# A fused attention and two MLPs: the second MLP's first chunk without the seven-product form, and a weight decoded between the two halves of a pair

## The chip, the cores and the metric

The kernel runs on one core of one Trainium2 chip. The metric is the device time of one execution in microseconds; three runs of the kernel before gave 1170.4 to 1173.76 us, median 1173.32 us. Lower is better.

## The reference

Attention with rotary embedding over 4 x 8 heads of 576 x 64, then two MLPs on the 2304 x 512 result. All of it is float32. What matters here are the MLPs:

```python
def _moe_ref(x, w_gate, w_val, w_out):        # 512 -> 1536 -> 512
    gate = 1.0 / (1.0 + np.exp(-(x @ w_gate)))
    val = x @ w_val
    return (gate * val @ w_out).astype(np.float32)

def _moe2_ref(x, w_in, w_out):                # 512 -> 2048 -> 512
    h = x @ w_in
    g = h * (1.0 / (1.0 + np.exp(-1.702 * h)))
    return (g @ w_out).astype(np.float32)
```

## The kernel before

The weights come from memory as 64-bit floats, seen as pairs of 32-bit words. Every float32 operand of a matmul is split into a high and a low part, and each product is made of three matmul sweeps (low by high, high by low, high by high; `split_mm`, L545).

**Tiles and chunks.** The 2304 tokens are five blocks n = 0 to 4: four of 512 and one of 256. Each MLP runs over chunks of 256 hidden columns (`FFC`): the first MLP has six chunks, (1, 0) to (1, 5), the second eight, (2, 0) to (2, 7). In a chunk, a block has a hidden step ("h", `hidden`, 48 matmuls in the first MLP, which has a gate and a value matrix, 24 in the second) and an output step ("2", `second`, 24 matmuls of 512 columns; 12 for the last block in the second MLP, or 24 of 256 columns in the first), whose results VectorE adds into `acc[n]` from four PSUM buffers (`ps_o`). `out1` (L702) is the first MLP's output step, `out2` (L721) the second's. In the last chunk of the first MLP `out1` also makes the next MLP's input of each block, with ScalarE for the high part and GpSimd for the low one (`split_x`, L105).

**Pairs.** Blocks 0 and 1 of a chunk are made together ("P" for the gate, or for the second MLP's only matrix, and "Q" for the value) by a seven-product form of a 2 x 2 block product (`hidden_pair`, L627): 7 products of 6 matmuls instead of 48 matmuls. It needs four sums of blocks 0 and 1 (`pair_sums`, L610: four VectorE operations on 1024 columns, four ScalarE copies, four VectorE low parts), made once per MLP, and differences of weights (`differences`, L199, on GpSimd; their casts on ScalarE and GpSimd are held back in the list `ready` until "r", or until a pair, takes them). Chunk (1, 0) makes its blocks plainly; all others pair. After its last product a pair still has a tail on VectorE and ScalarE (`step`, L659) that ends in the parts of `g` that the output steps read.

**Weights.** Each decode ("d", L929) takes the next piece (128 x 512 values, 512 KB as loaded) of a single list over all chunks: ScalarE (L182), five VectorE operations (L189 to L195), GpSimd for the low part (L217), then the issue of the next load. There is one `raw` buffer (L158), so that load waits until VectorE has read the old piece (L191). A chunk of the first MLP has 4 input pieces and 2 of w_out, one of the second 2 and 2. `w_out` of the first MLP has one buffer, so it can be decoded only when the last output step of the chunk before has been made.

**Order.** All engines work strictly in the order of the program text. The order of a chunk is written out as a string in `plans` (L967), where "s" does not occur yet:

```python
1: "P 2 Q d d h 2 d h d 2 r h d 2 d 2",
"last": "P 2 Q d d h 2 d h d 2 r h 2 d 2",
"first": "P 2 d h 2 d h 2 d h r d 2 d 2",
2: "P 2 d h 2 d h r 2 d h 2 d 2",
```

"last" is chunk (1, 5), "first" is (2, 0). Output steps wait in a queue, `pend`: "2" takes the oldest. At the start of each paired chunk one is left over from the chunk before, that of block 4, and the "2" behind P takes that one. `pair_sums` for the second MLP is called in `out1` right after block 1 of chunk (1, 5) (L719). The new `acc` of the second MLP comes from the same four buffers as the old one, and takes one whose old tile nothing will read again.

Of the kernel before, what the change touches and what calls it, by code (L numbers as in the profile page):

```python
# [11 lines left out]
AF = mybir.ActivationFunctionType  # L12
ALU = mybir.AluOpType
# [3 lines left out]
P = 128  # L17
# [9 lines left out]
def f(ap):  # L27
    return ap.bitcast(F32)
# [3 lines left out]
def attention_then_mlps(  # L32
# [20 lines left out]
    nc = tc.nc  # L53
# [5 lines left out]
    KT = DM // P  # L59
# [21 lines left out]
    first = keep.tile([P, 2 * KT * BLK], F32, tag="xhl0", name="first", bufs=1)  # L81
# [12 lines left out]
    xf = {}  # L94
    acc = {}

    def new_xhl(n):
        xhl[n] = mlp["x", (n + 1) // 2].tile([P, 2, KT, width[n]], F32R, tag=f"xhl{n}", name=f"xhl{n}", bufs=1)

    def new_f32(n, name):  # L100
        return big.tile(
            [P, KT * width[n]], F32, tag=f"f32_{width[n]}", name=f"{name}{n}", bufs=width.count(width[n])
        )

    def split_x(n, e, src, eng):  # L105
        a = src.rearrange("p (e w) -> p e w", w=width[n])[:, e, :]
        nc.scalar.activation(xhl[n][:, 0, e, :], a, AF.Copy)
        eng.tensor_tensor(xhl[n][:, 1, e, :], a, f(xhl[n][:, 0, e, :]), ALU.subtract)
# [17 lines left out]
    class Weights:  # L126
# [37 lines left out]
        def decode(self, i, act=False):  # L164

            if i < self.n_in and i % 2 == 0:
                self.w[i // 2] = self.half(big if i else self.pool, i // 2)
            if i >= self.n_in and self.o is None:  # L170
                where, tag = (big, "w_in1") if self.kind == 2 and self.c % 2 == 0 else (big, "w_out")
                self.o = where.tile([P, 2, MT * DM], F32R, tag=tag, name="w_out", bufs=1)
            w, at = (self.w[i // 2], i % 2) if i < self.n_in else (self.o, i - self.n_in)
            w = w[:, :, at * PIECE : (at + 1) * PIECE]
            raw = self.raw.pop(i)
            low, high = raw[:, :, 0], raw[:, :, 1]
            c = stage[0].tile([P, PIECE], U32, tag="wc", name="wc", bufs=1)
            t = stage[0].tile([P, PIECE], U32, tag="wt", name="wt")
            self.t[i] = t
            V = nc.vector  # L180
            return [
                lambda: nc.scalar.activation(f(c), f(high), AF.Copy, scale=2.0**-112),  # L182
                (
                    lambda: V.scalar_tensor_tensor(
                        f(c), f(c), LARGEST, least[:, 0:1].to_broadcast([P, PIECE]), op0=ALU.min, op1=ALU.max
                    )
                )
                if act
                else lambda: V.tensor_scalar(f(c), f(c), LARGEST, -LARGEST, op0=ALU.min, op1=ALU.max),  # L189
                lambda: V.tensor_scalar(t, c, 3, 0x7FFFFFF8, op0=ALU.logical_shift_left, op1=ALU.bitwise_and),  # L190
                lambda: V.scalar_tensor_tensor(t, low, 29, t, op0=ALU.logical_shift_right, op1=ALU.bitwise_or),  # L191
                lambda: V.scalar_tensor_tensor(t, c, 0x80000000, t, op0=ALU.bitwise_and, op1=ALU.bitwise_or),  # L192
                (lambda: nc.scalar.activation(w[:, 0, :], f(t), AF.Copy))
                if act
                else lambda: V.tensor_copy(w[:, 0, :], f(t)),  # L195
                lambda: self.lo(w, t),
            ] + ([lambda: self.differences(i // 2)] if i % 2 == 1 and i < self.n_in and (self.kind, self.c) != (1, 0) else [])

        def differences(self, m):  # L199
            t = [f(self.t.pop(2 * m + i)) for i in range(2)]  # L200
# [344 lines left out]
    def split_mm(ps, l, r, n):  # L545

        for sl, sr in ((1, 0), (0, 1), (0, 0)):
            for a in range(n):
                nc.tensor.matmul(  # L549
                    ps, l(sl, a), r(sr, a), start=(sl == 1 and a == 0), stop=(sl + sr == 0 and a == n - 1)  # L550
                )
# [49 lines left out]
    def pair_todo(at):  # L601
        a, b = (at[n].rearrange("p (h c) -> p h c", h=2) for n in range(2))
        return (
            ("S1", b[:, 1], b[:, 0], b[:, 1], ALU.add),
            ("S3", b[:, 0], a[:, 0], b[:, 0], ALU.subtract),
            ("S2", a[:, 0], b[:, 1], a[:, 0], ALU.subtract),
            ("S4", a[:, 1], a[:, 1], a[:, 0], ALU.subtract),
        )

    def pair_sums(todo):  # L610
        to = []
        for name, out_, x, y, op in todo:
            nc.vector.tensor_tensor(out_, x, y, op)
            if name == "S3":
                sums[:] = [mlp["s"].tile([P, 2, 6, BLK], F32R, tag="sums", name="sums", bufs=1)]
            t, e = (xhl[1], 0) if name == "S1" else (sums[0], 2 * "S2 S3 S4".split().index(name))
            to.append(t[:, :, e : e + 2, :].rearrange("p s e c -> p s (e c)"))
            nc.scalar.activation(to[-1][:, 0], out_, AF.Copy)
        for (_, x, *_), t in zip(todo, to):
            nc.vector.tensor_tensor(t[:, 1], x, f(t[:, 0]), ALU.subtract)  # L620

    def pair_room(kind):
        if kind == 1:
# [56 lines left out]
    def hidden(kind, W, n):  # L680
        g = mlp["p"].tile([P, 2, MT, BLK], F32R, tag="g", name="g", bufs=3)[:, :, :, : width[n]]
        for m in range(MT):
            hidden_m(kind, W, n, m, g)
        return g

    row_runs = []
    for t in range(NT // P):
        runs = []
        c = 0
        while c < P:  # L690
            b, j = divmod(t * P + c, S)
            if j < MAIN:
                ch, p0 = divmod(j, P)
                n = min(P - c, P - p0)
                runs.append((c, n, b * S + MAINC * p0 + ch, MAINC))
            else:
                n = min(P - c, S - j)
# [4 lines left out]
    def out1(c, nchunk, W, n, g):  # L702
        if c == 0:
            acc[n] = new_f32(n, "acc")
        wd = width[n]
        if c == nchunk - 1:
            new_xhl(n)
        for e in range(KT):
            ps = mlp["ps_o"].tile([P, 512], F32, tag="pso", name="pso")
            split_mm(ps[:, :wd], lambda s, m: W.w_out(s, m, e * P, P), lambda s, m: g[:, s, m, :], MT)  # L710
            a = acc[n].rearrange("p (e w) -> p e w", w=wd)[:, e, :]
            if c == 0:
                nc.vector.tensor_copy(a, ps[:, :wd])
            else:
                nc.vector.tensor_tensor(a, ps[:, :wd], a, ALU.add)  # L715
            if c == nchunk - 1 and (n != 1 or e >= KT // 2):
                split_x(n, e, acc[n], nc.gpsimd)
        if c == nchunk - 1 and n == 1:
            pair_sums(pair_todo(acc))  # L719

    def out2(c, nchunk, W, n, g):  # L721
        if c == 0:
# [123 lines left out]
    def split_block(n):  # L846
        for e in range(KT):
            if (n, e) not in split_done:
                split_e(n, e)

    with tc.manual_schedule():
# [72 lines left out]
        def next_load():  # L924
            if stream:
                key, i = stream[0]
                wts[key].load(i)
# [17 lines left out]
        for n in range(NBLK):  # L945
            if n + 1 < NBLK:
                split_block(n + 1)
            if n == 0:
                for i in range(W.done, W.n):
                    if i not in W.raw:  # L950
                        W.load(i)
                    for op in W.decode(i):
                        op()
                next_load()
            g = hidden_rest(W) if n == 0 else hidden(1, W, n)
            if n == 1:
                pair_sums(pair_todo(xf))
            if n == 4:
                ready.pop()()
                decode()  # L960
            if n:
                second()
            put(1, 0, n, g)
            if n > 1:
                decode()

        plans = {  # L967
# [4 lines left out]
        }  # L972
        for kind, c in chunks[1:]:
            W = wts[kind, c]
            plan = {(1, FF1 // FFC - 1): "last", (2, 0): "first"}.get((kind, c), kind)
            n = 2
            for op in plans[plan].split():
                if op == "r":
                    while ready:
                        ready.pop()()  # L980
                elif op == "P":
                    room = pair_room(kind)
                if op in "PQ":
                    for m, g in enumerate(hidden_pair(kind, W, "PQ".index(op), room)):
                        put(kind, c, m, g)
                elif op == "2":
                    second()
                elif op == "d":
                    decode()
                elif op == "h":  # L990
                    put(kind, c, n, hidden(kind, W, n))
                    n += 1
# [110 lines left out]
```

## Time and profile before

| | us |
|---|---|
| median of three runs | 1173.32 |
| the profiled execution, its time | 1172.27 |
| the same, its span | 1170.1 |
| TensorE busy (5988 matmuls) | 1115.5 (95%) |
| VectorE busy | 826.6 (71%) |
| ScalarE busy | 463.7 (40%) |
| GpSimd busy | 350.5 (30%) |

The span runs from the first to the last instruction. The attention comes first; chunk (1, 1) begins at 358.33 us, the second MLP at 767.93 us and its second chunk at 828.70 us. A TensorE busy time counts matmuls at either clock, so that a slow stretch is busy too. Times in the rows below are us from the span's start; a row of the timeline may stand for several instructions of a kind (x48).

### The profile page before, as it was taken

The page shows a single profiled execution, that of the slowest core. Times are in us where ns is not written, and L with a number is a line of the kernel's source. Part 1 is how long each engine was busy: PE and PEld are TensorE (multiplying, and loading weights), DVE is VectorE, ACT ScalarE, POOL GpSimd, SP SyncE. Part 2 cuts the span into 40 slices and gives each one's busy share as a digit, 9 for nine tenths or more (in the row PEclk, how much of TensorE's full clock was granted, in tenths as well). Part 3 has the DMA queues.
Part 4 walks back from the last instruction along what each step waited for, and adds up shares of the span by engine and source line. Part 5 has one row for each costly group of instructions (what it writes and reads, how often), then busy time and mean ns, then how long its engine had stood idle before and what let it go on. Part 6 is the DMA issues. An engine that isn't in the chain of part 4 may idle for free.

```text
span 1170.1 us, 15833 instructions
## 1 busy us (share of the span) xinstructions
PE 1115.5 (95%) x5988; PEld 926.4 (79%) x5988; DVE 826.6 (71%) x1418; ACT 463.7 (40%) x929; POOL 350.5 (30%) x333
## 2 busy tenths in 40 slices
PE   8999999999998899899998998698999999999998
PEld 7778888887787788787787887577788888888887
DVE  7887887877775656565556565676787777787864
ACT  5777877775522222222222222342223333243321
POOL 5445455412315032140130323352131230321300
PEclk9999999999999899899898998899899999999999
DMA  6676667621101110110111101011121111211114
GB/s 210 179 211 169 196 173 193 152 58 55 37 20 53 36 55 18 54 54 19 54 36 37 44 29 55 18 33 40 48 61 37 37 54 37 54 37 37 54 36 127
DMA packets 35804, 85.05 MB, mean 73 GB/s; under 512 B 6289, under 2 KB 11025, under 8 KB 33937
## 3 DMA queue, kind: packets, MB, share of 16 engines
q1 hardware_dynamic: 34912, 83.33, 24.8%
q8 instruction: 47, 0.77, 0.3%
q10 hardware_dynamic: 816, 0.72, 0.2%
q14 instruction: 29, 0.23, 0.1%
HBM read 60.44 MB, written 4.72 MB: 56 GB/s over the span
## 4 chain that ended last, share of the span: by engine, by line
PE 74%; DVE 13%; POOL 3%; ACT 3%; DMA 3%; issue 2%; SPq 0%; DVEq 0%; ACTq 0%; POOLq 0%
PE pso L549 25%; PE psh L549 16%; PE psh L636 14%; PE ps_x L518 5%; PE ps_p L487 4%; PE pss L415 4%; PE pss L416 3%; POOL wt L205 2%; DMA raw<-in_moe_w_out_dram 2%; DVE wt L191 2%; DVE g L671 1%; DVE wt L192 1%; PE ps_x L515 1%; DVE wc L189 1%; DVE wt L190 1%
## 5 line engine op out<-in xcount | busy, mean ns | idle before, releaser
L549 PE MATMUL psh<-xhl,w_in 128*128 128x512 f32 (+1 forms) x1488 | 293.1, 355 | 2.5 <-ACT gf L579 2.5
L549 PEld LDWEIGHTS psh<-xhl,w_in 128*128 128x128 f32 x1488 | 248.5, 189 | 43.2 <-ACT gf L579 3.0
L549 PE MATMUL pso<-w_out,g 128*128 128x512 f32 (+1 forms) x870 | 205.9, 393 | 8.0 <-DVE acc L732 5.8
L549 PEld LDWEIGHTS pso<-w_out,g 128*128 128x128 f32 x870 | 164.6, 191 | 43.4 <-DVE acc L732 6.2
L549 PE MATMUL pso<-g,w_out 128*128 128x512 f32 (+1 forms) x720 | 169.7, 394 | 30.7 <-POOL w_out L217 18.3
L549 PEld LDWEIGHTS pso<-g,w_out 128*128 128x128 f32 x720 | 135.7, 204 | 61.0 <-POOL w_out L217 20.4
L217 POOL TENSOR_TENSOR w_in<-wt,w_in 128x512 fp32r<-128x512 f32 x38 | 49.2, 1294 | 362.9 <-DVE w_in L195 334.8
L418 DVE TENSOR_REDUCE nm<-pss 128x1 f32<-128x576 f32 x144 | 108.4, 753 | 31.1 <-PE pss L416 30.2
L433 ACT ACTIVATE P<-pss,nm 128x576 f32<-128x576 f32 x128 | 94.8, 741 | 48.5 <-DVE nm L418 34.3
L581 ACT ACTIVATE g<-gf 128x512 fp32r<-128x512 f32 (+1 forms) x88 | 49.6, 564 | 154.6 <-DVE gf L580 152.9
L582 DVE TENSOR_TENSOR g<-gf,g 128x512 fp32r<-128x512 f32 (+1 forms) x88 | 60.0, 681 | 55.5 <-ACT g L581 55.5
L217 POOL TENSOR_TENSOR w_out<-wt,w_out 128x512 fp32r<-128x512 f32 x28 | 36.0, 1285 | 209.6 <-DVE w_out L195 209.6
L579 ACT ACTIVATE gf<-psh 128x512 f32<-128x512 f32 (+1 forms) x88 | 45.9, 522 | 116.4 <-PE psh L549 116.3
L734 DVE TENSOR_TENSOR acc<-pso,acc 128x512 f32<-128x512 f32 (+1 forms) x127 | 80.7, 680 | 11.5 <-PE pso L549 10.7
L580 DVE TENSOR_TENSOR gf<-psh,gf 128x512 f32<-128x512 f32 (+1 forms) x88 | 52.8, 600 | 48.4 <-PE psh L549 29.0
L305 POOL TENSOR_TENSOR x<-x,rope_sb 128x576 f32<-128x576 f32 x56 | 78.3, 1419 | 3.7 <-DMA x<-in_qk_dram 3.7
L487 PE MATMUL ps_p<-ident,P 128*128 128x128 f32 x576 | 78.4, 275 | 0.0
L715 DVE TENSOR_TENSOR acc<-pso,acc 128x512 f32<-128x512 f32 (+1 forms) x100 | 59.2, 632 | 21.1 <-PE pso L549 21.0
L487 PEld LDWEIGHTS ps_p<-ident,P 128*128 128x128 f32 x576 | 65.6, 141 | 8.0 <-issue 6.3
L182 ACT ACTIVATE wc<-raw 128x512 f32<-128x512 f32 x66 | 43.5, 659 | 69.8 <-DMA raw<-in_moe_w_out_dram 33.6
L518 PE MATMUL ps_x<-PT,v 128*64 128x320 f32 (+1 forms) x512 | 69.4, 412 | 0.0
L473 ACT ACTIVATE PT<-ps_p 128x512 f32<-128x512 f32 (+2 forms) x126 | 64.2, 534 | 4.4 <-PE ps_p L487 4.3
(124 smaller groups left out, 1726.7 us busy)
## 6 DMA issues: line engine op xcount, KB each, us to landing
x<-in_qk_dram SPq DMA_DIRECT2D x14, 1152.0 KB, 5.8
raw<-in_moe_w_out_dram SPq DMA_DIRECT2D x28, 512.0 KB, 3.5
raw<-in_moe_w_in_dram SPq DMA_DIRECT2D x16, 512.0 KB, 3.7
raw<-in_moe_w_val_dram SPq DMA_DIRECT2D x12, 512.0 KB, 3.9
raw<-in_moe_w_gate_dram SPq DMA_DIRECT2D x10, 512.0 KB, 3.8
v<-in_v_dram SPq DMA_DIRECT2D x16, 256.0 KB, 3.5
Z<-X SPq DMA_DIRECT2D x14, 288.0 KB, 3.0
Z<-Y SPq DMA_DIRECT2D x14, 288.0 KB, 3.7
```

What stands on the lines that cost most here:

```text
L217: nc.gpsimd.tensor_tensor(w[:, 1, :], f(t), f(w[:, 0, :]), ALU.subtract)
L305: eng.tensor_tensor(x, x, rope_sb[:, t, c * S : (c + 1) * S], ALU.mult)
L418: nc.vector.tensor_reduce(nm, ps[:, :, :HALF], axis=AX.XY, op=ALU.max, negate=True)
L433: nc.scalar.activation(st[i]["P"][j][:, c : c + S].rearrange("p (n c) -> p n c", n=2), ps[:, :, :HALF], AF.Exp, bias=nm, accum_out=st[i][" ...
L473: nc.scalar.activation(dst, src, AF.Copy)
L487: nc.tensor.transpose(ps[:, (2 * x + y) * P : (2 * x + y + 1) * P], st[i]["P"][2 * a + y][:, c * P : (c + 1) * P], ident,)
L518: nc.tensor.matmul(ps[h * D : (h + 1) * D, :n], vt[:, h * MAINC + t, :], PT[:, h * (MAINC + 1) + t, :], start=False, stop=(t == MAINC - 1),)
L549: nc.tensor.matmul(ps, l(sl, a), r(sr, a), start=(sl == 1 and a == 0), stop=(sl + sr == 0 and a == n - 1))
L582: nc.vector.tensor_tensor(g[:, 1, m, :], gf, f(g[:, 0, m, :]), ALU.subtract)
L636: nc.tensor.matmul(ps, W.block(i, w, sl, kk), pair_x(x, sr, kk), start=start and first, stop=end, skip_group_check=not start,)
L715: nc.vector.tensor_tensor(a, ps[:, :wd], a, ALU.add)
L734: nc.vector.tensor_tensor(a, ps, a, ALU.add)
```

## The change

Chunk (2, 0) makes blocks 0 and 1 by plain hidden steps, so it needs no weight differences (the condition in `decode`: `self.c` instead of all but (1, 0)). `pair_sums` becomes a generator in five steps: "s" in the plan of (2, 0) takes one. `out1` no longer calls it, and splits all four parts of block 1. Where chunk (1, 0) decodes the pieces of (1, 1) is moved up by half a block. In chunks (1, 1) to (1, 5) one decode of the own w_out moves from behind Q to before it, and the second one stays behind it. Chunk (1, 5) decodes one piece more, without "r"; chunk (2, 0) has six "2" instead of five.

```diff
@@ -194,7 +194,7 @@
                 if act
                 else lambda: V.tensor_copy(w[:, 0, :], f(t)),
                 lambda: self.lo(w, t),
-            ] + ([lambda: self.differences(i // 2)] if i % 2 == 1 and i < self.n_in and (self.kind, self.c) != (1, 0) else [])
+            ] + ([lambda: self.differences(i // 2)] if i % 2 == 1 and i < self.n_in and self.c else [])
 
         def differences(self, m):
             t = [f(self.t.pop(2 * m + i)) for i in range(2)]
@@ -607,17 +607,21 @@
             ("S4", a[:, 1], a[:, 1], a[:, 0], ALU.subtract),
         )
 
-    def pair_sums(todo):
-        to = []
-        for name, out_, x, y, op in todo:
+    def pair_sums(at):
+        low = None
+        for name, out_, x, y, op in pair_todo(at):
             nc.vector.tensor_tensor(out_, x, y, op)
             if name == "S3":
                 sums[:] = [mlp["s"].tile([P, 2, 6, BLK], F32R, tag="sums", name="sums", bufs=1)]
             t, e = (xhl[1], 0) if name == "S1" else (sums[0], 2 * "S2 S3 S4".split().index(name))
-            to.append(t[:, :, e : e + 2, :].rearrange("p s e c -> p s (e c)"))
-            nc.scalar.activation(to[-1][:, 0], out_, AF.Copy)
-        for (_, x, *_), t in zip(todo, to):
-            nc.vector.tensor_tensor(t[:, 1], x, f(t[:, 0]), ALU.subtract)
+            t = t[:, :, e : e + 2, :].rearrange("p s e c -> p s (e c)")
+            nc.scalar.activation(t[:, 0], out_, AF.Copy)
+            if low:
+                nc.vector.tensor_tensor(*low)
+            low = t[:, 1], out_, f(t[:, 0]), ALU.subtract
+            yield
+        nc.vector.tensor_tensor(*low)
+        yield
 
     def pair_room(kind):
         if kind == 1:
@@ -713,10 +717,8 @@
                 nc.vector.tensor_copy(a, ps[:, :wd])
             else:
                 nc.vector.tensor_tensor(a, ps[:, :wd], a, ALU.add)
-            if c == nchunk - 1 and (n != 1 or e >= KT // 2):
+            if c == nchunk - 1:
                 split_x(n, e, acc[n], nc.gpsimd)
-        if c == nchunk - 1 and n == 1:
-            pair_sums(pair_todo(acc))
 
     def out2(c, nchunk, W, n, g):
         if c == 0:
@@ -954,30 +956,38 @@
                 next_load()
             g = hidden_rest(W) if n == 0 else hidden(1, W, n)
             if n == 1:
-                pair_sums(pair_todo(xf))
-            if n == 4:
+                for _ in pair_sums(xf):
+                    pass
+            elif n == 2:
+                decode()
+            elif n == 3:
                 ready.pop()()
+            elif n == 4:
                 decode()
             if n:
                 second()
             put(1, 0, n, g)
-            if n > 1:
+            if n in (2, 3):
                 decode()
 
         plans = {
-            1: "P 2 Q d d h 2 d h d 2 r h d 2 d 2",
-            "last": "P 2 Q d d h 2 d h d 2 r h 2 d 2",
-            "first": "P 2 d h 2 d h 2 d h r d 2 d 2",
+            1: "P 2 d Q d h 2 d h d 2 r h d 2 d 2",
+            "last": "P 2 d Q d h 2 d h d 2 h d 2 d 2",
+            "first": "h 2 h s 2 s d h s 2 d h s r 2 d h s 2 d 2",
             2: "P 2 d h 2 d h r 2 d h 2 d 2",
         }
         for kind, c in chunks[1:]:
             W = wts[kind, c]
             plan = {(1, FF1 // FFC - 1): "last", (2, 0): "first"}.get((kind, c), kind)
-            n = 2
+            n = 0 if c == 0 else 2
+            if c == 0:
+                made = pair_sums(acc.copy())
             for op in plans[plan].split():
                 if op == "r":
                     while ready:
                         ready.pop()()
+                elif op == "s":
+                    next(made)
                 elif op == "P":
                     room = pair_room(kind)
                 if op in "PQ":
```

## Rows read from the trace of the kernel before

**Rows 1.** The page, part 1: engine, busy us (share of the span), instructions.

```profile
PE 1115.5 (95%) x5988; PEld 926.4 (79%) x5988; DVE 826.6 (71%) x1418; ACT 463.7 (40%) x929; POOL 350.5 (30%) x333
```

**Rows 2.** Waits of TensorE: line, whom for, us in total, times, longest.

```profile
PE pso L549 <- POOL w_out L217: 18.3, 5, 3.7
...
PE pso L549 <- DVE acc L715: 12.4, 5, 10.2
...
PE pso L549 <- DVE acc L732: 5.8, 1, 5.8
```

**Rows 3.** Timeline, TensorE and VectorE, chunk (1, 1): start, us, engine, line, operation [idle <-releaser].

```profile
358.33 1.52 PE L636 MATMUL psh<-xhl,w_in 128*128 128x512 f32 x6
...
367.01 0.68 DVE L648 TENSOR_TENSOR u<-psh,u 128x512 f32<-128x512 f32 x1
...
372.96 3.04 PE L549 MATMUL pso<-g,w_out 128*128 128x256 f32 x24
```

**Rows 4.** Timeline, TensorE, output of block 0, first and last of five chunks.

```profile
396.26 0.39 PE L549 MATMUL pso<-g,w_out 128*128 128x512 f32 x1
...
400.23 8.24 PE L549 MATMUL pso<-g,w_out 128*128 128x512 f32 x23 [3.58 <-POOL w_out L217]
...
408.31 11.04 PE L549 MATMUL psh<-xhl,w_in 128*128 128x512 f32 x48
...
419.19 5.60 PE L549 MATMUL pso<-g,w_out 128*128 128x512 f32 x24
...
710.74 0.39 PE L549 MATMUL pso<-g,w_out 128*128 128x512 f32 x1
...
722.60 11.04 PE L549 MATMUL psh<-xhl,w_in 128*128 128x512 f32 x48
```

**Rows 5.** Window of 10 us: busy of PE, PEld, DVE, ACT, POOL; clock; DMA share, GB/s.

```profile
400.00:410.00 10.00, 9.77 (x31) 7.86 (x32) 5.41 (x9) 1.79 (x4) 0.18 (x1) 0.70 0.09 32
```

**Rows 6.** Timeline, ScalarE and GpSimd, chunk (1, 1), the two pieces of w_out.

```profile
393.03 1.29 POOL L217 TENSOR_TENSOR w_out<-wt,w_out 128x512 fp32r<-128x512 f32 x1 [18.96 <-DVE w_out L195]
...
395.26 0.66 ACT L182 ACTIVATE wc<-raw 128x512 f32<-128x512 f32 x1 [5.32 <-DMA raw<-in_moe_w_out_dram]
...
398.91 1.27 POOL L217 TENSOR_TENSOR w_out<-wt,w_out 128x512 fp32r<-128x512 f32 x1 [4.59 <-DVE w_out L195]
```

**Rows 7.** Timeline, TensorE, last outputs of chunk (1, 5), and first pair after.

```profile
744.67 5.63 PE L549 MATMUL pso<-g,w_out 128*128 128x512 f32 x24
...
760.49 7.60 PE L549 MATMUL pso<-g,w_out 128*128 128x512 f32 x24 [10.20 <-DVE acc L715]
...
767.93 1.52 PE L636 MATMUL psh<-xhl,w_in 128*128 128x512 f32 x6
```

**Rows 8.** The line of the sums' low parts: ns min/median/max, first and last start.

```profile
L620 DVE TENSOR_TENSOR sums<-acc,sums x3: 1219/2277/2285, 751.7 to 755.1; 128x1024 fp32r<-128x1024 f32 x3
```

**Rows 9.** Timeline, all engines, end of chunk (2, 0).

```profile
819.93 2.48 DVE L732 COPY acc<-pso 128x512 f32<-128x512 f32 x4
...
820.67 8.20 PE L549 MATMUL pso<-w_out,g 128*128 128x512 f32 x24 [5.77 <-DVE acc L732]
...
828.70 1.52 PE L636 MATMUL psh<-xhl,w_in 128*128 128x512 f32 x6
```

**Rows 10.** Groups of lines on VectorE: busy us, mean ns, idle before.

```profile
L582 DVE TENSOR_TENSOR g<-gf,g 128x512 fp32r<-128x512 f32 (+1 forms) x88 | 60.0, 681 | 55.5 <-ACT g L581 55.5
...
L580 DVE TENSOR_TENSOR gf<-psh,gf 128x512 f32<-128x512 f32 (+1 forms) x88 | 52.8, 600 | 48.4 <-PE psh L549 29.0 <-ACT gf L579 18.7
```

**Rows 11.** Timeline, TensorE and VectorE, end of the pair of chunk (2, 3).

```profile
933.78 2.88 PE L549 MATMUL pso<-w_out,g 128*128 128x512 f32 x12
...
933.23 1.28 DVE L671 TENSOR_TENSOR g<-room,g 128x512 fp32r<-128x512 f32 x2
...
935.82 0.69 DVE L671 TENSOR_TENSOR g<-room,g 128x512 fp32r<-128x512 f32 x1
...
936.50 5.60 PE L549 MATMUL psh<-xhl,w_in 128*128 128x512 f32 x24
```

## The prediction

> **What bounds the kernel now.** Begin with the page's first part: TensorE is busy 95% of the span [rows 1], so only what shortens its work or its waits counts. The table of its waits names what is left in the MLPs: five waits for a decoded w_out, one of 10.2 us and one of 5.8 us for VectorE's sums into `acc` [rows 2]. A wait costs more than its idle time, so the timeline is read next, from the start of one step to the start of the next. The undisturbed pace is 48 matmuls in 419.19 - 408.31 = 10.88 us, 0.2267 us each, 5.44 us for a step of 24 [rows 4]. The output step behind the value's pair took 408.31 - 396.26 = 12.05 us in the first paired chunk and 11.86 in the fifth [rows 4]: 3.6 us idle (and one matmul), and then 23 matmuls in 8.24 us. [...]
>
> **Term 1, the own w_out: -32.5 us.** In the five chunks both pieces were decoded behind Q. GpSimd finished the first at 394.32, and the second could not begin before its load, which waits for the only `raw` buffer: ScalarE got it at 395.26, GpSimd ended at 400.18, and TensorE had wanted it from 396.26 on [rows 4, 6]. A decode is thus 398.91 - 395.92 = 2.99 us of VectorE and 1.27 of GpSimd. With the first piece before Q, its load is in place since the chunk before, and the second's load runs beside Q's 42 matmuls (9.52 us); the second takes the old place of the first and ends 2 us before TensorE's 396.26. What queues behind the moved decode are Q's additions on VectorE; that engine has nothing else until two products of Q are done (2.7 us), so they come under 0.6 us late, and the product that needs them is the sixth of seven. I take nothing for that; without this cover it is 3 us a chunk. w_out's buffer is free, as P's output step lies before. Five steps of 11.95 us become 5.44: 5 x 6.5 = 32.5. Low end 15 (the second piece still late by 2 us and the clock falling all the same, 3.5 a chunk), high end 33.
>
> **Term 2, the start of chunk (1, 1): -5.1 us.** Its first pair took 372.96 - 358.33 = 14.63 us instead of 42 x 0.2267 = 9.52, because its addition into u stood behind two late decodes on VectorE, at 367.01 [rows 3]. Moved up by half a block, the fourth piece is decoded beside block 4's hidden and the output of block 3; by the lengths above its five operations end at about 357.5, the copies of block 3's output 2.5 later, and P's second product ends 12 matmuls (2.7 us) behind 358.33, at 361. The moved loads and GpSimd's differences only come earlier. Bounds 0 and 5.1; nearest the upper.
>
> **Term 3, the end of the first MLP: -12.1 us.** Two output steps took 767.93 - 744.67 = 23.26 us instead of 10.88 [rows 7]: 12.4 lost, since the sums (twelve operations on VectorE and ScalarE) stood before block 4's hidden and so before the additions that free the PSUM buffers. Without them VectorE frees the first buffer about when it is wanted; I leave 0.3 us. The two more parts of block 1 to split and the added decode fall to ScalarE and GpSimd, which lose the differences. Bounds 9 and 12.4.
>
> **Term 4, chunk (2, 0): -3.0 us.** Before: 828.70 - 767.93 = 60.8 us [rows 7, 9], and block 4's output (12 matmuls, 2.7 us) was left to the next chunk: 63.5 for the same work. After, TensorE has 4.5 hidden steps, 4.5 output steps and the old block 4 (half a step): 9.5 x 5.44 = 51.7, six matmuls more than the pair. But VectorE becomes the bound. A hidden step costs it 2 x (0.60 + 0.68 + 0.63 waiting for ScalarE, 55.5/88) = 3.8 [rows 10], 4.5 blocks with the dearer short one 17.7; copies 2.48 a block [rows 9], with the old block 4 12.6; four decodes 11.9; eight operations on 1024 columns at 1.22 [rows 8], 9.8; one overlap with GpSimd 1.1. That is 53.1, and it starts about 6 us late: first come the copies of the last output of (1, 5), ready only when that step is over, behind a decode that GpSimd's splits slow, and ScalarE's four split copies. So TensorE waits twice for the copies, before the outputs of blocks 2 or 3 and of block 4, with a fall of the clock; I walk this to about 60.5. Bounds 51.7 (no wait) and 69 (every sum overlapped).
>
> **Term 5, what goes wrong: +28 us.** The plan of (2, 0) now has six "2". Before it the queue holds one output step and five are put in, so it is empty at the end. In all seven later chunks the "2" behind P was the old block 4's, and those 2.72 us (936.50 - 933.78) covered the pair's tail. Now it takes the output of block 0 of the same chunk, at once. The tail in the trace: TensorE is through the pair at 933.78; the low part of g for block 0's first half is ready at 934.51 (the second of two operations from 933.23), that for its second half at 936.51 [rows 11]. An output step begins with these two. So TensorE waits 0.7, does one matmul, and waits until 2.7: 2.6 us idle, where the trace of before has none. What the clock does then I bound: nothing, or what it lost after longer waits: 2.8 us after 3.6 [rows 4], 2.0 after 10.2 (7.60 against 5.60, rows 7, 4), 2.6 after 5.8 [rows 9]. I take the middle, 1.3, with 0.1 for the restart: 4.0 x 7 = 28. Ends 7 x 2.5 = 17.5 and 7 x 5.4 = 38. A gain is excluded, since the matmuls are the same. Nothing else waits in these chunks: the outputs of blocks 3 and 4 now end the chunk, and VectorE is through with them by P's second product.
>
> **Sum.** -32.5 - 5.1 - 12.1 - 3.0 + 28.0 = -24.7. From the profiled 1172.27 (span 1170.1 and 2.2 around it) that is 1147.6; the profiled run lay 1.05 below the median of 1173.32, so 1149.
>
> **A rule against the change.** One of the three low parts took 1219 ns and two 2277 and over [rows 8]; beside the slow ones GpSimd was casting weight differences. [...]
>
> **Rivals.**
> - The clock holds through 2.6 us of idle: only the wait counts, 7 x 2.6 = 18, time 1139. For it: the wait is shorter than any that I have seen cost 2 us or more. Against: it is mostly one gap. 17%.
> - All eight operations of the sums meet GpSimd: 8 x 1.06 = 8.5 more in (2, 0), where VectorE is the bound: 1157. Against: GpSimd has only some 20 us of work in those 60. 8%.
> - The change does half of what it says: the second w_out piece stays late, 17 us of term 1 remain: 1166. Against: the 2 us of room. 6%.
> - The pair's tail is covered after all, or the queue isn't empty: no term 5, 1121. I find nothing that covers it. 4%.
> - [...] 5%.
>
> My forecast keeps 60%; its own range is 1137 to 1162. The range for 8 in 10 takes in the first two rivals and the ends of terms 4 and 5: 1132 to 1164. A difference of 0.3% (3.5 us) is what runs of this kernel can tell from none. Faster: all but the last rival and mixtures of several misses, 92%; within 0.3% 2%; slower 6%.
>
> **What would show it.** Term 1: no wait for L217 before the outputs of block 0 in chunks (1, 1) to (1, 5), five steps of 5.44. Term 2: the first pair of (1, 1) in 9.5 us. Term 3: no 10 us gap before the last output of (1, 5). Term 4: waits for L732 in (2, 0), VectorE above 85% there. Term 5: seven waits for L671 in TensorE's table, 2.5 us each, and a chunk of the second MLP at about 51.8 instead of 47.8 us. Were that table empty of L671, the forecast would be wrong by its largest doubtful term; were the period above 55, the sign is in question.

## The result, and the profile after

The kernel after takes 1140.64 us (median of four runs, 1140.49 to 1145.01), the one before 1173.26 in the same comparison: ratio 0.9736, 95% interval 0.9708 to 0.9764. That is 32.6 us faster; 1149 had been predicted, within 1132 to 1164, so the range held and the forecast was 8.4 us too high. The profiled execution of after has a span of 1138.7 us, 31.4 less than that of before.

First the page, part 1, of the kernel after; it answers to [rows 1]:

```profile
PE 1103.9 (97%) x5994; PEld 917.5 (81%) x5994; DVE 820.2 (72%) x1413; ACT 462.9 (41%) x928; POOL 346.7 (30%) x329
```

The six matmuls more are the plain pair of (2, 0), as worked out. TensorE is busy 11.6 us less all the same: less of its work runs at the low clock (its mean granted clock is 0.994, and was 0.975). Its waits, beside [rows 2] (after the change, line 675 is line 671 of before, 719 is 715 and 734 is 732):

```profile
PE pso L549 <- DVE g L675: 14.8, 14, 1.5
PE pso L549 <- DVE acc L734: 5.0, 2, 3.8
...
PE pso L549 <- DVE acc L719: 2.1, 4, 0.6
```

The 18.3 us for w_out and the 10.2 us for the sums are gone. In their place are 14 waits that before did not have, two in each of seven chunks (the first line); the two waits of the second line are in (2, 0), and the four of the third were there before. The timeline of TensorE in the kernel after (start, us, engine, line, operation) answers to [rows 3, 4, 7]: the first pair of (1, 1), block 0's output in it, and the end of (1, 5).

```profile
358.07 1.52 PE L640 MATMUL psh<-xhl,w_in 128*128 128x512 f32 x6
...
367.60 3.04 PE L549 MATMUL pso<-g,w_out 128*128 128x256 f32 x24
...
390.89 5.60 PE L549 MATMUL pso<-g,w_out 128*128 128x512 f32 x24
396.33 11.04 PE L549 MATMUL psh<-xhl,w_in 128*128 128x512 f32 x48
...
706.73 11.10 PE L549 MATMUL pso<-g,w_out 128*128 128x512 f32 x48
717.67 2.66 PE L549 MATMUL psh<-xhl,w_in 128*128 128x512 f32 x11
```

The pair takes 367.60 - 358.07 = 9.53 us (14.63 before), block 0's output 5.44 (12.05 before), the last two outputs of (1, 5) 10.94 (23.26 before), all without a wait. The window of 10 us that answers to [rows 5] (PE busy, its clock, DMA share, GB/s) is now full, at a granted clock of 1.00; in the trace of before the clock was 0.50 in that window up to 406 us and 1.00 from 407 on:

```profile
400.00:410.00 10.00, 10.00 (x46) 1.00 0.15 52
```

Where the change costs time is the second MLP. Chunk (2, 0) of after, timeline of all engines, beside [rows 8, 9]:

```profile
756.25 4.93 POOL L205 TENSOR_TENSOR wt<-wt 128x256 f32<-128x256 f32 x4
...
760.49 1.76 DVE L620 TENSOR_TENSOR sums<-acc,sums 128x1024 fp32r<-128x1024 f32 x1
...
762.18 2.47 DVE L734 COPY acc<-pso 128x512 f32<-128x512 f32 x4
...
762.91 5.75 PE L549 MATMUL pso<-w_out,g 128*128 128x512 f32 x24 [1.23 <-DVE acc L734]
...
772.47 5.49 PE L549 MATMUL pso<-w_out,g 128*128 128x512 f32 x12 [3.81 <-DVE acc L734]
...
777.75 0.51 PE L640 MATMUL psh<-xhl,w_in 128*128 128x512 f32 x1
```

It lasts 777.75 - 717.67 = 60.08 us and has two waits for VectorE's copies, of 1.23 and 3.81 us. Behind the second, twelve matmuls take 5.49 us, at a granted clock of 0.50; at 1.00 they take 2.88 [rows 11]. The operation of the sums at 760.49 meets GpSimd's weight differences (756.25) and takes 1.76 us. And the tail of a pair, the same place as [rows 11], in chunk (2, 1) of after, with the fourth of the seven below it:

```profile
786.06 1.52 PE L640 MATMUL psh<-xhl,w_diff 128*128 128x512 f32 x6
786.87 1.28 DVE L675 TENSOR_TENSOR g<-room,g 128x512 fp32r<-128x512 f32 x2
...
788.21 0.50 PE L549 MATMUL pso<-w_out,g 128*128 128x512 f32 x1 [0.63 <-DVE g L675]
789.45 0.69 DVE L675 TENSOR_TENSOR g<-room,g 128x512 fp32r<-128x512 f32 x1
...
790.20 5.51 PE L549 MATMUL pso<-w_out,g 128*128 128x512 f32 x23 [1.49 <-DVE g L675]
...
939.63 0.50 PE L549 MATMUL pso<-w_out,g 128*128 128x512 f32 x1 [0.62 <-DVE g L675]
941.62 7.11 PE L549 MATMUL pso<-w_out,g 128*128 128x512 f32 x23 [1.49 <-DVE g L675]
```

Both have the same two waits. Behind the first, 23 matmuls take 5.51 us, behind the other 7.11. The windows over these two outputs (PE busy, clock) show why: 1.00 of full speed in the one, 0.83 in the other.

```profile
790.00:800.00 10.00, 9.80 (x43) 1.00 0.06 13
...
940.00:950.00 10.00, 8.52 (x31) 0.83 0.01 2
```

Of the seven pairs, five are followed by a step of 5.51 or 5.55 us, and two (941.62 and 1044.14) by one of 7.11 and 7.12.

### The profile page after: what moved, and what is told of

Read it like the earlier page. It is cut to its first block, busy times and chain, and to the rows that moved or that the text cites. A ratio compares the mean times of both kernels' runs of the same rounds, so it can differ in the third digit from the quotient of the medians.

```text
span 1138.7 us, 15823 instructions
## 1 busy us (share of the span) xinstructions
PE 1103.9 (97%) x5994; PEld 917.5 (81%) x5994; DVE 820.2 (72%) x1413; ACT 462.9 (41%) x928; POOL 346.7 (30%) x329
## 4 chain that ended last, share of the span: by engine, by line
PE 82%; DVE 11%; ACT 3%; POOL 2%; issue 1%; DMA 1%; SPq 0%; DVEq 0%; ACTq 0%; POOLq 0%
PE pso L549 25%; PE psh L549 23%; PE psh L640 13%; PE ps_x L518 5%; PE ps_p L487 5%; PE pss L415 4%; PE pss L416 3%; PE ps_x L515 1%; DVE g L675 1%; POOL wt L205 1%; DVE wt L191 1%; ACT g L581 1%; DVE gf L580 1%; DVE nm L418 1%; DVE wt L192 1%
## 5 line engine op out<-in xcount | busy, mean ns | idle before, releaser
L549 PE MATMUL psh<-xhl,w_in 128*128 128x512 f32 (+1 forms) x1536 | 304.3, 356 | 2.6 <-ACT gf L579 2.6
L549 PEld LDWEIGHTS psh<-xhl,w_in 128*128 128x128 f32 x1536 | 257.5, 189 | 45.1 <-ACT gf L579 3.0
L549 PE MATMUL pso<-w_out,g 128*128 128x512 f32 (+1 forms) x870 | 210.3, 398 | 19.8 <-DVE g L675 14.8
L217 POOL TENSOR_TENSOR w_in<-wt,w_in 128x512 fp32r<-128x512 f32 x38 | 49.3, 1296 | 372.2 <-DVE w_in L195 344.2
L549 PE MATMUL pso<-g,w_out 128*128 128x512 f32 (+1 forms) x720 | 153.3, 369 | 2.1 <-DVE acc L719 2.1
L549 PEld LDWEIGHTS pso<-g,w_out 128*128 128x128 f32 x720 | 125.5, 189 | 26.3 <-DVE acc L719 3.8
L581 ACT ACTIVATE g<-gf 128x512 fp32r<-128x512 f32 (+1 forms) x92 | 52.2, 567 | 144.7 <-DVE gf L580 143.0
L582 DVE TENSOR_TENSOR g<-gf,g 128x512 fp32r<-128x512 f32 (+1 forms) x92 | 66.2, 720 | 58.3 <-ACT g L581 58.3
L736 DVE TENSOR_TENSOR acc<-pso,acc 128x512 f32<-128x512 f32 (+1 forms) x127 | 84.0, 682 | 29.0 <-PE pso L549 27.5
L580 DVE TENSOR_TENSOR gf<-psh,gf 128x512 f32<-128x512 f32 (+1 forms) x92 | 55.8, 606 | 63.4 <-PE psh L549 36.4
L217 POOL TENSOR_TENSOR w_out<-wt,w_out 128x512 fp32r<-128x512 f32 x28 | 36.3, 1296 | 190.6 <-DVE w_out L195 190.6
L719 DVE TENSOR_TENSOR acc<-pso,acc 128x512 f32<-128x512 f32 (+1 forms) x100 | 59.0, 630 | 10.3 <-PE pso L549 10.2
L205 POOL TENSOR_TENSOR wt<-wt 128x256 f32<-128x256 f32 x68 | 57.5, 845 | 4.0
```

The source lines that it names most:

```text
L205: nc.gpsimd.tensor_tensor(dst, x, y, ALU.subtract)
L217: nc.gpsimd.tensor_tensor(w[:, 1, :], f(t), f(w[:, 0, :]), ALU.subtract)
L549: nc.tensor.matmul(ps, l(sl, a), r(sr, a), start=(sl == 1 and a == 0), stop=(sl + sr == 0 and a == n - 1))
L580: nc.vector.tensor_tensor(gf, pss[-1][:, :wd], gf, ALU.mult)
L582: nc.vector.tensor_tensor(g[:, 1, m, :], gf, f(g[:, 0, m, :]), ALU.subtract)
L736: nc.vector.tensor_tensor(a, ps, a, ALU.add)
```

## Experiments

Times vary from execution to execution. In the profiled executions whose program is the same up to the second MLP, that MLP begins between 717.67 and 720.93 us, and the kernel before took 1163.76 to 1173.74 us in the runs of the experiments. So where an effect is small, lengths of one stage are compared and not only totals. Only one execution of each kernel is profiled. "Hidden start" is the start of the first hidden step behind a pair; without a loss, one chunk of the second MLP is 47.78 us.

### One output step is kept in the queue

The kernel after, where the plan of (2, 0) doesn't take the last "2":

```diff
-            "first": "h 2 h s 2 s d h s 2 d h s r 2 d h s 2 d 2",
+            "first": "h 2 h s 2 s d h s 2 d h s r 2 d h s 2 d",
```

> The changed kernel with the last output step taken out of the plan of chunk (2, 0), so that the output of block 4 stays in the queue and is again the step behind each pair. Theory (the uncovered tail of the pair costs the seven chunks of the second MLP 22.0 us, five of them 2.7 and two 4.3): these seven waits for g vanish and their period returns to 47.8 us; chunk (2, 0) loses the 3.8 us wait before block 4's output, but VectorE is then late for the first pair, so that only some 3 us of it are won. Time 1140.6 - 22 - 3 = 1116, between 1111 and 1119. Rival (the seven waits only move VectorE's backlog about, since its share of the chunk is over 75%): other waits take their place, time above 1132.

Measured: 1118.25 us (1115.99 to 1119.84), ratio to before 0.9557 (0.9525 to 0.9589). Its waits of TensorE:

```profile
PE psh L640 <- DVE gf L655: 3.1, 1, 3.1
...
PE pso L549 <- DVE acc L719: 2.2, 4, 0.6
PE pso L549 <- DVE acc L734: 1.2, 1, 1.2
```

No wait for `g` is left, and the hidden starts of (2, 2) and (2, 3) are 883.13 - 835.36 = 47.77 us apart. So the seven tails were the empty queue and nothing else: one "2" in one plan string costs 22 us (the total is 22.4 less, although the second MLP began 3.1 us later here, at 720.78; the difference is what (2, 0) and the first pair behind it gain). The 3.81 us wait for block 4's copies is gone too, since that output now follows the pair; in its place the first pair of (2, 1) waits 3.1 us for an addition that stands behind a decode on VectorE.

### The own w_out alone

The kernel before with only the moved decode in (1, 1) to (1, 5):

```diff
-            1: "P 2 Q d d h 2 d h d 2 r h d 2 d 2",
-            "last": "P 2 Q d d h 2 d h d 2 r h 2 d 2",
+            1: "P 2 d Q d h 2 d h d 2 r h d 2 d 2",
+            "last": "P 2 d Q d h 2 d h d 2 r h 2 d 2",
```

> The kernel before with one edit: in chunks (1, 1) to (1, 5) one decode of w_out stands before Q instead of behind it. Theory (term 1 is 6.5 us a chunk and owes nothing to the other edits): 1173.3 - 32.5 = 1140.8, no wait of TensorE for L217 left, the chunk period 72.05 us instead of 78.65. Rival (part of the gain came from the pieces of chunk (1, 1) that are decoded earlier, or a wait moves to Q): 1150 to 1160, with waits for L217 or in the pair.

Measured: 1142.22 us (1139.39 to 1142.87), ratio 0.9759 (0.9726 to 0.9792); the span is 30.5 us shorter than before's. Block 0's output in (1, 1):

```profile
396.66 5.60 PE L549 MATMUL pso<-g,w_out 128*128 128x512 f32 x24
402.10 2.20 PE L549 MATMUL psh<-xhl,w_in 128*128 128x512 f32 x9
```

5.44 us again, and no wait for L217 before these five steps. The second MLP begins at 736.67 instead of 767.93: 31.3 less, which is 32.5 less 0.4 for a longer attention and 0.9 for a longer fall of the clock behind the 10.2 us wait, which this kernel still has (24 matmuls in 8.49 us, 7.60 in before). So one moved decode is worth as much as the whole change; the rest of the change gains some 20 us and loses them again.

### The pieces of (1, 1) earlier, alone

The kernel before with only the decodes of (1, 0) moved up by half a block:

```diff
+            elif n == 2:
+                decode()
+            elif n == 3:
                 ready.pop()()
+            elif n == 4:
                 decode()
...
-            if n > 1:
+            if n in (2, 3):
                 decode()
```

> The kernel before with only the order of the decodes in chunk (1, 0) changed (a decode ahead of the outputs of blocks 1, 2 and 3, none behind block 4's). Theory: the first pair of (1, 1) takes about 9.5 us instead of 14.6 and nothing else moves, so 5.1 us less than the kernel before, ratio 0.9956. Rival: VectorE's decodes that now stand behind block 2's copies delay the output of block 3 or 4, and at most 1 to 2 us are left.

Measured: 1165.14 us (1160.76 to 1167.03) against 1171.10, ratio 0.9957 (0.9934 to 0.998). The timeline of its first pair in (1, 1), and of two of its five waits for w_out:

```profile
359.15 1.52 PE L636 MATMUL psh<-xhl,w_in 128*128 128x512 f32 x6
...
362.53 0.68 DVE L648 TENSOR_TENSOR u<-psh,u 128x512 f32<-128x512 f32 x1
...
368.67 3.04 PE L549 MATMUL pso<-g,w_out 128*128 128x256 f32 x24
...
396.00 5.51 PE L549 MATMUL pso<-g,w_out 128*128 128x512 f32 x23 [3.64 <-POOL w_out L217]
...
706.70 5.51 PE L549 MATMUL pso<-g,w_out 128*128 128x512 f32 x23 [3.69 <-POOL w_out L217]
```

The addition into u begins 3.4 us behind the pair's start instead of 8.7 [rows 3], and the pair takes 9.52 us. For the pair the theory holds to the tenth; the totals are 6.0 us apart (2.3 to 7.7 by the interval), which can't tell 5.1 from a little more or less. The two profiled spans are 8.7 us apart, and the last two lines show the main reason why it is more: this kernel still has all five waits for w_out, of 3.58 to 3.93 us, but behind two of them the clock did not fall. Its five steps took 53.5 us in sum, those of before 59.7 (the first and the last of them are in [rows 4]), where the clock fell behind all five.

### The first half of g first

The kernel after; in the seven later chunks block 0's output runs all four rows over the first half of `g`, into four PSUM buffers, before the second half is wanted:

```diff
+        if n == 0 and c > 0:
+            halves = [mlp["ps_o"].tile([P, 512], F32, tag="pso", name="pso") for _ in range(4)]
+            for m in range(MT):
+                for t in range(4):
+                    for x, (sl, sr) in enumerate(((1, 0), (0, 1), (0, 0))):
...
```

> The changed kernel, where the output step of block 0 in chunks (2, 1) to (2, 7) makes the products with the first half of g for all four rows of tiles first (12 matmuls, 2.7 us) and then those with the second half. Theory (the wait is first for the low part of the first half, 0.6 us, and then for the second half, 1.5 us, ready 2.0 us later): only the first is left, 0.6 to 0.8 us a pair, no fall of the clock: 1140.6 - 7 x 1.9 - 2 x 1.6 = 1124, between 1121 and 1127. Rival (an output step waits for all of g, or VectorE's additions then come late since four buffers are ready at once): 1138 or above.

Measured: 1126.33 us (1124.36 to 1127.18), ratio 0.9622 (0.9585 to 0.9659). One pair of it:

```profile
790.48 5.73 PE L733 MATMUL pso<-w_out,g 128*128 128x512 f32 x24 [0.63 <-DVE g L675]
796.05 4.24 PE L549 MATMUL psh<-xhl,w_in 128*128 128x512 f32 x18
```

The 1.49 us waits are gone and the 0.63 us ones are left, all seven without a fall of the clock; the hidden starts are 48.7 us apart, 0.9 a pair lost instead of 2.7 to 4.3. So the order in which TensorE takes the tail's results is most of its price.

### The second half of g later

The kernel after, with the tail's last operations in another order, so that the second half of `g` is ready 1.2 us later:

```diff
-            (2, 3), (3, 1), (2, 4), (3, 2), (3, 3), (3, 4),
+            (2, 3), (3, 1), (3, 2), (2, 4), (3, 3), (3, 4),
```

> The changed kernel, where in the tail of every pair one VectorE operation of the last quarter (which itself waits for ScalarE) stands before the low part of block 0's second half. This holds back the second half of g by about 1.4 us behind each pair of the second MLP; the pairs of the first MLP have a hidden step behind them and should not feel it. Theory (what a fall of the clock costs comes on top of the wait, and a longer wait makes it fall more often): waits of 2.9 instead of 1.5 us, 7 x 1.4 = 10 us more, and falls behind most of the seven pairs instead of two, 1.6 us or more each: 1153 to 1160. Rival (the clock falls as seldom as before, two of seven): 1150 to 1151.

Measured: 1161.57 us (1157.2 to 1162.39), ratio 0.9929 (0.9896 to 0.9962). Two of its seven tails:

```profile
791.36 7.10 PE L549 MATMUL pso<-w_out,g 128*128 128x512 f32 x23 [2.66 <-ACT g L673]
...
1003.86 8.40 PE L549 MATMUL pso<-w_out,g 128*128 128x512 f32 x23 [2.66 <-DVE g L675]
```

The seven steps take 7.10, 5.51, 7.11, 8.30, 8.40, 6.84 and 7.14 us: the clock falls behind six of seven pairs and each fall costs 1.3 to 2.9. The wait is 7 x 1.17 = 8.2 us longer in sum, the falls cost 11.8 in place of 3.2; together 16.8, and the two profiled spans (1155.4 and 1138.7) are 16.7 apart. The other four executions of this kernel lie 4 to 5 us above its profiled one, at a mean clock of 0.980 or 0.979 instead of 0.984, so that the median lies 1.6 us above the range expected: the direction was right, and the price of the falls was taken too low.

### One gap instead of two

The kernel after, where block 0's first row takes the second half of `g` first, so that no matmul stands between the two waits:

```diff
+                x = n == t == 0 < c
...
+                    lambda s, m: g[:, s, m ^ x, t * P : (t + 1) * P],
+                    lambda s, m: W.w_out(s, m ^ x, e, w),
```

> The kernel after, where the first of block 0's four output rows in the seven later chunks of the second MLP takes the second half of g first. So no matmul stands between the two waits (0.63 and 1.49 us in the kernel after): one gap of about 2.4 us, the same matmuls. Theory 1: what the pair costs is the idle time in sum, and whether the clock falls does not hang on the one matmul: falls behind 2 to 4 of 7 pairs as there, time 1139 to 1144. Theory 2: the one matmul keeps the clock up, and the prediction's 1.3 us a pair would have been right for a single gap: falls behind 6 or 7 pairs, 1.6 us each, 6 to 8 us more, time 1147 to 1150.

Measured: 1145.91 us (1144.02 to 1147.89), ratio 0.9799 (0.9776 to 0.9822). Two of its seven steps:

```profile
897.67 5.78 PE L549 MATMUL pso<-w_out,g 128*128 128x512 f32 x24 [2.61 <-DVE g L675]
948.40 7.21 PE L549 MATMUL pso<-w_out,g 128*128 128x512 f32 x24 [2.61 <-DVE g L675]
```

Three steps take 5.73 to 5.78 us and four 7.21 to 7.38. The time lies between the two theories: one gap of 2.61 us is followed by a fall four times in seven, at 1.5 to 1.6 each. Four of seven here and two of seven in after, in one execution each, don't tell whether the single matmul matters. It doesn't decide alone: with it two of seven waits are followed by a fall, and without it three of seven are not.

### The sums in one lump

The kernel after with the five steps of the sums one behind the other:

```diff
-            "first": "h 2 h s 2 s d h s 2 d h s r 2 d h s 2 d 2",
+            "first": "h 2 h s s s s s 2 d h 2 d h r 2 d h 2 d 2",
```

> The kernel after with the five steps of the sums in (2, 0) in one lump behind the hidden of block 1 instead of spread. Theory: VectorE's total in (2, 0) bounds that chunk, so where the sums stand moves the waits and not the end: TensorE waits some 5 to 8 us early, for block 0's copies, and the two later waits (1.2 and 3.8 us) go; (2, 0) takes 58 to 63 us against 60.1, time 1138 to 1144. Rival: the spreading is what matters; a lump of about 10 us on VectorE comes on top with a fall of the clock, (2, 0) takes 67 us or more, time 1148.

Measured: 1140.77 us (1140.42 to 1142.29), ratio 0.9754 (0.9713 to 0.9795): the same as after. TensorE in (2, 0), its two waits and its end:

```profile
744.98 5.73 PE L549 MATMUL pso<-w_out,g 128*128 128x512 f32 x24 [1.87 <-DVE acc L734]
...
772.73 3.06 PE L549 MATMUL pso<-w_out,g 128*128 128x512 f32 x12 [2.81 <-DVE acc L734]
775.63 1.52 PE L640 MATMUL psh<-xhl,w_in 128*128 128x512 f32 x6
```

(2, 0) takes 775.63 - 718.28 = 57.35 us, 2.7 less than in after: one wait came early, but of 1.9 us instead of the 5 to 8 expected, a late one of 2.8 us stayed, and no fall of the clock follows either. What is gained there is lost in the later chunks, whose tails are the same (0.62 and 1.49 us) and yet are followed by four steps of 7.01 to 7.13 us instead of two. That the sums are spread is worth nothing here; what counts is that they no longer stand at the end of (1, 5), which holds for both kernels.

### A version that beats both

The kernel with one output step kept in the queue, and half of the copies out of PSUM in (2, 0) on ScalarE:

```diff
-                    nc.vector.tensor_copy(a, ps)
+                    copy(t % 2 == 0, a, ps)
```

> The kernel after with one output step left in the queue at the end of (2, 0), and every second copy out of PSUM in (2, 0) moved from VectorE to ScalarE. Theory: VectorE is what bounds (2, 0); it loses 9 copies of 0.68 us there, so the waits for its copies and the 3.1 us wait in the first pair of (2, 1) go, 4 to 6 us less than the version that only leaves the output step in the queue (1118): 1111 to 1114. Rival: ScalarE is late with the shares of hidden that VectorE waits for, and it gains under 2 us: 1116 or more.

Measured: 1113.57 us (1112.72 to 1114.03), ratio 0.9518 (0.9478 to 0.9558). Its waits that answer to those of the first experiment:

```profile
PE pso L549 <- DVE acc L719: 2.2, 4, 0.6
PE psh L640 <- DVE gf L655: 1.8, 1, 1.8
```

The time is as expected, the way there only in part. From the start of (2, 0) to the end of the first pair behind it take 60.97 us instead of 63.73: 2.8 less, since of the 3.1 us wait 1.8 are left and the 1.2 us wait for copies is gone with its restart. Another 1.5 us are an earlier start of the second MLP, at 719.33 instead of 720.78, and that is nearly all luck: behind one and the same wait in chunk (1, 0) the clock fell in the execution of the first experiment and not in this one (48 matmuls in 12.55 and 11.17 us).

Then, in (1, 1) to (1, 4), the last decode moves behind the last output:

```diff
-            1: "P 2 d Q d h 2 d h d 2 r h d 2 d 2",
+            1: "P 2 d Q d h 2 d h d 2 r h 2 d 2 d",
```

> As the one before it, and in the chunks (1, 1) to (1, 4) the last decode stands behind the last output instead of ahead of it. Theory: the four waits of 0.55 us for the additions of the last output go, with what the clock loses behind them some 0.75 us each: 3 us less, 1108 to 1111. Rival: the decode is then late for the next chunk's first pair, whose addition into u stands behind it, and it gains nothing or loses 1 to 3 us.

Measured: 1111.02 us (1109.62 to 1112.73), ratio 0.9502 (0.9453 to 0.9551). The four waits of 0.55 us are gone and a chunk takes 71.24 instead of 72.06 us, four times 0.8; the medians are 2.6 us apart. This is the best version: 29.6 us below the kernel after and 60 below the one before, with TensorE busy 99% of the span and a mean clock of 0.998. A last step, the decode behind 1.8 us of wait moved into the next chunk, lost:

```diff
-            "first": "h 2 h s 2 s d h s 2 d h s r 2 d h s 2 d",
+            "first": "h 2 h s 2 s d h s 2 d h s r 2 d h s 2",
+            "next": "P d 2 d h 2 d h r 2 d h 2 d 2",
```

> As the version with the copies shared and the last decode of (1, 1) to (1, 4) moved, and the last decode of (2, 0) moved behind the pair of (2, 1). Theory: the 1.8 us wait in the first pair of (2, 1), whose addition into u stood behind that decode on VectorE, goes, 2 to 2.5 us less: 1107 to 1110. Rival: the decode then holds up the additions of the old block 4's output, or is late for block 0's output, and as much is lost there.

Measured: 1116.65 us (1114.9 to 1116.7), ratio 0.9544 (0.952 to 0.9568). One row of (2, 1) has it:

```profile
812.81 8.51 PE L549 MATMUL pso<-w_out,g 128*128 128x512 f32 x24 [3.71 <-DVE acc L736]
```

The pair and the half output behind it got 2.1 us shorter, but now every later decode of that chunk runs later, and one stands before the additions of block 2's output, which free the buffers that block 3's output waits for: 3.7 us of wait with a fall of the clock cost 6.8 us, and a short wait of 0.15 us for w_out before block 0's output another 0.5. The rival was right that as much is lost, and more; of the two places that it named, block 0's output was the small one, and the main loss lies in neither.

## Why the prediction was right, and where it was off

- **What bounds.** Right: everything that moved the time is a wait of TensorE or its clock.
- **Term 1, -32.5.** Right: five steps of 5.44. The second piece is ready on GpSimd at 388.89, the 2.0 us before TensorE's start (390.89) that were worked out. Alone it shortens the first MLP by 31.3 us. That the size holds to the tenth owes something to luck: it was taken from one execution of before, in which the clock fell behind all five waits, and is compared with the same execution; in the run with the pieces earlier the same five steps took 53.5 us and not 59.7, and from there the term would have been 26.3.
- **Term 2, -5.1.** Right: 14.63 to 9.53, and 9.52 by itself.
- **Term 3, -12.1.** Right: 12.3, as not even the 0.3 us left for the first buffer were needed.
- **Term 4, -3.0.** Right in size (60.08 instead of the walked 60.5) and in mechanism: two waits for the copies, where they had been put. VectorE is busy 49.4 of those 60.1 us, 82%, less than the 85% named as the sign. That TensorE waits for the copies since VectorE has too much to do is shown by the version with half of them on ScalarE, where (2, 0) has no wait for copies.
- **The sums beside GpSimd's work.** Of the eight operations of the sums two ran beside GpSimd's differences, at 758.81 and 760.49, and took 1.76 us each; the other six, beside which GpSimd had no operation, took about 1.22. So the price was 1.1 us, as the sum had it, and not 8.5. That the six would be slowed too if they met GpSimd is the author's estimate; no run here shows it.
- **Term 5, +28.** The mechanism was right and the size was off. The waits came in all seven chunks and in the two places named, and with one output step left in the queue they are gone. Measured are 22.2 us: 2.8 behind the first pair (17.79 us to the hidden start instead of 14.96), and 1101.57 - 795.54 = 306.0 us for six periods instead of 286.7. The term that was mis-sized is the clock: I took 1.3 us behind every pair, and it fell behind two of seven only, 1.6 us each, 0.46 a pair on average. That is 7 x 0.84 = 5.9 us, all of the 5.8 by which the term came out too high. The idle time was 2.1 instead of 2.6, and the restart, which is what a wait costs beside its idle time and without a fall, 0.55 instead of 0.1: these two cancel.
- **The sum.** -32.5 - 5.1 - 12.3 - 3.4 + 22.2 = -31.1, and 0.3 of a shorter attention: -31.4, the whole difference of the spans. Of the 8.4 us by which the forecast was too high, 5.8 are term 5, 0.9 the other terms and the attention, 1.3 the step from the span to the median (3.25 us were added, 1.9 were measured), and 0.4 rounding. The 32.6 us also rest on four runs of before at 1170.4 to 1173.76; in the three later comparisons its median was 1168.67 to 1171.10.
- **The rivals.** The first, that the clock holds through the idle time (1139, given 17%), came closer than the forecast; it isn't the truth either, as the clock fell twice. The others didn't come; a slower kernel would have had to lose at the seven tails more than the 53.3 us that the other terms gained, and 22.2 were lost there. What was wrong was to price a fall as a constant taken from longer waits (3.6 us and more, where in the trace of before each had been followed by one), instead of as a chance times a price. The prediction said of this rival that the wait is shorter than any that had cost 2 us or more. That overlooks waits of about this length that the trace of before has and its rows don't show: one in (2, 0), behind a single matmul as in the tails, with a fall, and one in (1, 0) without:

```profile
785.79 0.39 PE L549 MATMUL pso<-w_out,g 128*128 128x512 f32 x1
788.30 7.38 PE L549 MATMUL pso<-w_out,g 128*128 128x512 f32 x23 [2.12 <-DVE w_out L195]
...
298.02 11.17 PE L549 MATMUL psh<-xhl,w_in 128*128 128x512 f32 x48 [2.54 <-ACT gf L579]
```

Behind the first, 23 matmuls take 7.38 us, 1.9 more than the 5.51 of after's tails; behind the second, 48 take 11.17, against 11.04 without a wait. A third, of 2.17 us in the first pair of (1, 1), is followed by a fall too: 6 matmuls take 2.93 us, where they take 1.65 behind other waits. Both outcomes were there to be read before the change.

What stays open is what decides whether a fall follows: not the length of the waits alone, as the kernel after and the one with the lump have the same waits and two and four falls, and as the last three rows of the table below show for longer ones.

## What to carry to other kernels

When an edit changes what a queue holds at the end of a stage, count its entries once round the loop: here one "2" more in one plan string took the cover from the tail in seven later chunks, two thirds as much as the best part of the change gained. Price a TensorE wait as its idle time, plus its restart, plus a chance times the price of a fall of the clock (here 2.1, 0.55 and 0.46 us a pair), and take the chance from waits of that length, in more than one execution. Test each part of a bundle alone: one moved decode was worth the whole.

## What the hardware showed that was not expected

Whether the clock falls behind a wait can't be told from the length of the wait alone: within one execution, equal waits are followed by a fall in some chunks and not in others. These are the seven tails of one profiled execution of each kernel, and below them three sets of other waits:

| kernel | waits, us | steps behind them at a fallen clock | a fall costs, us |
|---|---|---|---|
| one step kept | none | 0 of 7 | |
| first half first | 0.63 | 0 of 7 | |
| after | 0.62 and 1.49 | 2 of 7 | 1.6 |
| sums in a lump | 0.62 and 1.49 | 4 of 7 | 1.5 to 1.6 |
| one gap | 2.61 | 4 of 7 | 1.5 to 1.6 |
| second half later | 0.63 and 2.66 | 6 of 7 | 1.3 to 2.9 |
| all twelve kernels, block 1's hidden in (1, 0) | 2.44 to 2.61 | 5 of 12 | 1.3 to 1.6 |
| before, five waits for w_out | 3.58 to 3.71 | 5 of 5 | 2.4 to 2.7 |
| pieces earlier, the same five | 3.58 to 3.93 | 3 of 5 | 1.6 to 2.4 |

The row of the twelve kernels says most, since they have one program up to that wait. Here it is in the kernel after and in the one of the first experiment:

```profile
297.76 11.18 PE L549 MATMUL psh<-xhl,w_in 128*128 128x512 f32 x48 [2.57 <-ACT gf L579]
...
299.50 12.55 PE L549 MATMUL psh<-xhl,w_in 128*128 128x512 f32 x48 [2.55 <-ACT gf L579]
```

The scatter from run to run goes with the clock too: of the kernel before in the runs of the experiments, the quickest execution (1163.76 us) has a mean clock of 0.985, and the three over 1173 us have 0.974. How often the clock fell in each isn't known, as they have no trace. In the run with the lump every second pair, from the first to the seventh, was followed by a fall (7.01 to 7.13 us for the 23 matmuls behind it, and 5.51 or 5.52 behind the others). That it hangs on when a wait comes is the author's guess from this: no run here shifted the waits alone.
